# Four small transposes moved into an earlier wait, one batch's attention units one group sooner, and another cut of a tile's lead groups

## The chip, the cores and the metric

One core of one Trainium2 chip. The metric is the device time of one execution in microseconds (us). Times are quoted as medians over executions. A "mean granted clock" stands beside every execution: the share of full speed that TensorE was granted over the span. 1.000 or 0.999 is called full clock here. The span that a profile shows is about 1.8 us shorter than the device time of the same execution.

## The reference, cut to what matters

```python
# retention attention: q, k, v are (8 batches, 8 heads, 576 positions, 64)
scores = scale * q @ k.T
ret    = scores * Dmat            # gamma[h] ** (i - j) for i >= j, else 0
x      = (ret @ v) as rows of 512 # 8 * 576 = 4608 tokens

# mixture of 4 experts, all of them for each token
p   = domain_probs / (domain_probs.sum(-1) + 1e-09)
out = sum over e of  p[:, e] * (relu(x @ w1[e]) @ w2[e])   # 512 -> 1024 -> 512
```

## The kernel before

The 4608 tokens are worked through in nine tiles of 512. A tile is a Python generator `moe(nt)`: for each of 4 experts it runs 8 "up" groups (w1, one group for 128 hidden rows) and 4 "po" groups (w2, one group for 128 tokens) and yields after each, so a tile has 48 groups, counted from 0. A table `plan` names what attention work of the next batch is emitted after which group. All TensorE work is one instruction stream in the order of emission; that order is what this change edits. A batch has 576 tokens, so tile 1 (tokens 512 to 1023) needs the last 64 tokens of batch 0 and the first 448 of batch 1, chunk by chunk of 128: `xT` of batch 1's chunk 3 must be there before tile 1's last columns.

```python
def mixing_weights():                       # after group 1 of tile 0
    pp = ps_at.tile([128, E, NTT], FP32, tag="at", name="pp")
    for e in range(E):
        nc.tensor.transpose(pp[:, e, :], probs_raw[:, :, e], identf)
    nc.vector.tensor_copy(probs, pp)
    ...                                     # normalise on VectorE

def moe(nt, lead=0):
    n0 = nt * NT
    ...
    for e in range(E):
        hT = hpool.tile([128, NFC, NT], BF16, tag="hT")
        for fc in range(NFC):
            if e == 0 and fc < lead:
                if fc == 0:
                    early = [ps_mm.tile([128, NT], FP32, tag="mm", name="ph") for _ in range(lead)]
                    for x in range(lead):
                        up(early[x], e, x, slice(0, NT // 2))
                        if x != 1:
                            yield
                ph = early[fc]
                up(ph, e, fc, slice(NT // 2, NT))
            ...
            nc.scalar.activation(hT[:, fc, :], ph, Relu)
            yield
        for ns in range(NSUB):
            po = ...                        # 8 matmuls over fc, needs all of hT and w2
            ...
            yield

# start of the program, after attention of batch 0 in four units:
    next(tile0)            # half groups of tile 0, wait for the first half of w1[0]
    a0.O(*UNITS[3])
    next(tile0)
    w20 = load_w2(0)       # the DMA of the first w2 is issued on POOL, in order with the casts
    late_constants()       # with identf, the 36x36 identity for the transposes
    ...
# tile 0: batch 1's chunks. Tc transposes q and k, kv updates the state,
# Sc computes scores, Oc the output and xT
    for c, g in enumerate((40, 42, 44, 46)):
        at(g, Tc(c))
        if c < 3: at(g + 1, kv(c), Sc(c))
        if c > 0: at(g + 1, Oc(c - 1))
    at(47, kv(3))
# after tile 0:
    Sc(3); next(tiles[1]); next(tiles[1])   # three half groups of tile 1
    Oc(3)
```

Of the kernel before, what the change touches and what calls it, by code (L numbers as in the profile page):

```python
# [9 lines left out]
FP32 = mybir.dt.float32  # L10
# [10 lines left out]
def kernel(  # L21
# [10 lines left out]
    nc = tc.nc  # L32
    B, H, S, D = q.shape
    N, E = moe_domain_probs.shape
# [10 lines left out]
    NT = 512  # L45
    n_nt = N // NT
    NSUB = NT // 128
    NTT = N // 128
    lg = [math.log(1.0 - 2.0 ** (-5.0 - h)) for h in range(H)]
    allp = list(range(NP))  # L50

    const = ctx.enter_context(tc.tile_pool(name="const", bufs=1))
# [6 lines left out]
    ps_mm = ctx.enter_context(tc.tile_pool(name="ps_mm", bufs=3, space=PSUM))  # L59
    ps_at = ctx.enter_context(tc.tile_pool(name="ps_at", bufs=4, space=PSUM))  # L60
# [12 lines left out]
    state = {}  # L73
# [20 lines left out]
    def load(b):  # L94
        load_alloc(b)
        for c in range(NCH):
            load_chunk(b, c)
        load_rem(b)
# [49 lines left out]
                   allow_small_or_imprecise_dtypes=True)  # L148
    ident = const.tile([128, 128], BF16)
    make_identity(nc, ident)  # L150

    tri2 = const.tile([128, 2, 128], BF16)
    nc.gpsimd.memset(tri2, 1.0)
# [1 line left out]
        nc.gpsimd.affine_select(out=tri2[j:j + 64], in_=tri2[j:j + 64], compare_op=mybir.AluOpType.is_ge,  # L155
                                fill=0.0, base=0, channel_multiplier=-2, pattern=[[-1, 2], [1, 128]])
    tri = const.tile([128, 128], BF16)
    identf = const.tile([NTT, NTT], FP32)

    def late_constants():  # L160
        nc.gpsimd.memset(tri, 1.0)
        nc.gpsimd.affine_select(out=tri, in_=tri, compare_op=mybir.AluOpType.is_ge, fill=0.0,
                                base=0, channel_multiplier=-1, pattern=[[1, 128]])
        nc.gpsimd.tensor_copy(identf, ident[:NTT, :NTT])

    lgp = const.tile([128, NP], FP32)
    for p in range(NP):
# [11 lines left out]
    def load_gq(pairs):  # L179
        for p in pairs:  # L180
            nc.scalar.activation(gq[:, p, :], pos_i, Exp, scale=lgp[:, p:p + 1], bias=lsc)
# [5 lines left out]
    probs = const.tile([128, E, NTT], FP32)  # L187
    psm = const.tile([128, NTT], FP32)

    def mixing_weights():  # L190
        pp = ps_at.tile([128, E, NTT], FP32, tag="at", name="pp")
        for e in range(E):
            nc.tensor.transpose(pp[:, e, :], probs_raw[:, :, e], identf)
        nc.vector.tensor_copy(probs, pp)
        nc.vector.tensor_reduce(psm, probs[:, :, :].rearrange("p e t -> p t e"),
                                axis=mybir.AxisListType.X, op=ADD)
        nc.vector.tensor_scalar_add(psm, psm, 1e-9)
        nc.vector.reciprocal(psm, psm)
        nc.vector.tensor_tensor(probs, probs, psm[:, :].unsqueeze(1).to_broadcast([128, E, NTT]), op=MULT)
# [260 lines left out]
                                        gq[:, 2 * u:2 * u + 2, ts], op=MULT)  # L460


    def moe(nt, lead=0):
        n0 = nt * NT

        def up(ph, e, fc, ts):
            for dc in range(NDC):
                nc.tensor.matmul(ph[:, ts], lhsT=w1_sb[e][:, dc, fc * 128:(fc + 1) * 128],  # L468
                                 rhs=xT[:, dc, n0 + ts.start:n0 + ts.stop], start=(dc == 0), stop=(dc == NDC - 1))

        acc = [apool.tile([128, Dm], FP32, tag="acc", name="acc") for _ in range(NSUB)]
# [4 lines that stand above are left out]
                    if fc == 0:  # L476
                        early = [ps_mm.tile([128, NT], FP32, tag="mm", name="ph") for _ in range(lead)]
                        for x in range(lead):
                            up(early[x], e, x, slice(0, NT // 2))
                            if x != 1:  # L480
                                yield
                    ph = early[fc]
                    up(ph, e, fc, slice(NT // 2, NT))
                else:
                    ph = ps_mm.tile([128, NT], FP32, tag="mm", name="ph")
                    up(ph, e, fc, slice(0, NT))
# [3 lines that stand above are left out]
                t = nt * NSUB + ns  # L490
                pe = probs[:, e, t:t + 1]
                last = t == NTT - 1 and e == E - 1
                w = Dm // 2 if last else Dm
                for d in range(0, Dm, w):
                    po = ps_mm.tile([128, w], FP32, tag="mm", name="po")
                    for fc in range(NFC):
                        nc.tensor.matmul(po, lhsT=hT[:, fc, ns * 128:(ns + 1) * 128],  # L497
                                         rhs=w2_sb[e][:, fc, d:d + w], start=(fc == 0), stop=(fc == NFC - 1))
                    a = acc[ns][:, d:d + w]
                    if e == 0:  # L500
                        nc.scalar.activation(a, po, Copy, scale=pe)  # L501
                    else:
                        nc.vector.scalar_tensor_tensor(a, po, pe, a, op0=MULT, op1=ADD)  # L503
                    if e == E - 1:
                        eng = nc.scalar if last and d // w % 2 else nc.sync
                        eng.dma_start(out=out[n0 + ns * 128:n0 + (ns + 1) * 128, d:d + w], in_=a)
                yield
# [2 lines left out]
    a0 = AttP(0)  # L510
    UNITS = [(hf, u) for hf in range(2) for u in range(2)]

    tiles = [moe(nt, lead=3 if nt < 2 else 0) for nt in range(n_nt)]
    tile0 = tiles[0]
    warm(8)
    for n, eng in (("k", nc.gpsimd), ("q", nc.scalar), ("v", nc.gpsimd)):
# [1 line left out]
    for x, (hf, u) in enumerate(UNITS):  # L518
        a0.T(hf, u, nc.scalar)
        if x < 2:  # L520
            load_gq((2 + x,))
        if x == 0:
            warm(4)
        else:
            a0.O(*UNITS[x - 1])
        if x < 3:
            a0.cast("k", *UNITS[x + 1], nc.gpsimd)
            a0.cast("q", *UNITS[x + 1], nc.gpsimd)
            if x:
                load_w1(0, x - 1)  # L530
            a0.cast("v", *UNITS[x + 1], nc.gpsimd)
        a0.S(hf, u)
        if x == 0:
            warm(2)
        a0.kv(hf, u)
    next(tile0)
    a0.O(*UNITS[3])
    next(tile0)
# [11 lines left out]
    for nt in range(n_nt):  # L550
        plan = {}

        def at(g, *fs):
            plan.setdefault(g, []).extend(fs)

        if nt == 0:
            at(1, mixing_weights)
            at(3, lambda: a0.cast_rem(nc.gpsimd))
            at(20, a0.Trem)
            at(22, a0.Srem)  # L560
            at(24, a0.Orem)
            def begin1():
                A = state["a1"] = Att(1)
                for c in range(NCH):
                    for n in "kqv":
                        A.cast(n, c, nc.gpsimd)
                    if c == 0:
                        load_chunk(1, 2)
                        load_chunk(1, 3)
                load_rem(1)  # L570
                load(2)

            at(25, begin1)
            for c, g in enumerate((40, 42, 44, 46)):
                at(g, lambda c=c: state["a1"].Tc(c))
                if c < 3:
                    at(g + 1, lambda c=c: state["a1"].kv(c, allp), lambda c=c: state["a1"].Sc(c))
                if c > 0:
                    at(g + 1, lambda c=c: state["a1"].Oc(c - 1))
            at(47, lambda: state["a1"].kv(3, allp))  # L580
        elif nt + 1 < B:
            if nt == 1:
                a1 = state["a1"]
                at(0, lambda: a1.cast_rem(nc.gpsimd))
                at(2, a1.Trem)
                at(4, a1.Srem)
                at(6, a1.Orem)
            def begin(b=nt + 1):
                A = state["A"] = Att(b)
                for c in range(NCH):  # L590
                    for n in "kqv":
                        A.cast(n, c, nc.gpsimd)
                A.cast_rem(nc.gpsimd)
                for c in range(NCH + 1):
                    A.dmaT(c)
                if b + 1 < B:
                    load(b + 1)

            at(7 if nt == 1 else 0, begin)
            for n, g in zip(range(NCH), (13, 15, 17, 18) if nt == 1 else (9, 11, 13, 15)):  # L600
                at(g, lambda n=n: state["A"].kv(n, allp))
            at(19 if nt == 1 else 17, lambda: state["A"].S([0, 1]))
            at(24, lambda: state["A"].Srem(), lambda: state["A"].O([0, 1]))
            at(27, lambda: state["A"].S([2, 3]))
            at(32, lambda: state["A"].O([2, 3], rem=True))
        for g, _ in enumerate(tiles[nt]):
            for f in plan.get(g, ()):
                f()
        if nt == 0:
            state["a1"].Sc(3)  # L610
            next(tiles[1])
            next(tiles[1])
            state["a1"].Oc(3)


# [28 lines left out]
```

## Time and profile before

| | us |
|---|---|
| device time, median of 3 | 563.56 |
| span of the profiled execution | 561.2 |
| TensorE busy (98% of the span) | 552.4 |
| TensorE stall before the first `po` (w2 landing) | 0.76 |
| TensorE stall for batch 1's last `xT` | 0.78 |

The list of what TensorE waited for, in the kernel before (what it was about to do, whom it waited for, total us, times, longest):

```profile
...
PE ph L468 <- DVE xT L316: 0.8, 1, 0.8
PE po L497 <- DMA wt_491<-in_moe_w_dram: 0.8, 1, 0.8
PE pt L391 <- POOL qm L381: 0.7, 1, 0.7
PE ph L468 <- DMA wt_268<-in_moe_w_dram: 0.7, 1, 0.7
...
PE kvp L236 <- ACT sbd L241: 0.4, 1, 0.4
```

The two lines left out are waits at the start (1.3 and 0.4 us). The list adds up to about 5 us of 561, so a change of the order alone can win little. The change aims at two of them: the one for the first weights (`wt_268`, as a place to put work) and the one for `xT`.

The chain of waits between 10 and 30 us (start, us, what), which tells what the first `po` depends on:

```profile
15.51 0.55 POOL vm L381
16.06 11.17 DMA wt_491<-in_moe_w_dram
...
27.28 2.76 PE po L497 x12
```

The first w2 (`wt_491`) is issued by POOL at 16.06, is on its way for 11.17 us, and the first `po` starts when it has landed. TensorE does not appear in the chain before 27.28. The same stretch in TensorE's timeline (start, us, engine, line, operation, output and inputs, count, and in brackets the idle time before and what ended it):

```profile
16.51 0.72 PE L412 MATMUL kvp<-vm,km 64*128 64x128 bf16 x8
17.92 0.61 PE L468 MATMUL ph<-xT,wt_268 128*128 128x256 bf16 x4 [0.69 <-DMA wt_268<-in_moe_w_dram]
...
21.00 0.67 PE L193 MATMUL pp<-identf,probs_raw 36*128 36x36 f32 x4
...
27.28 7.08 PE L497 MATMUL po<-wt_491,hT 128*128 128x512 bf16 x32 [0.76 <-DMA wt_491<-in_moe_w_dram]
```

And the end of tile 0, where the half groups of tile 1 (line 468, 256 columns), `Oc(3)` (lines 309 and 314) and the second halves meet:

```profile
83.00 1.48 PE L468 MATMUL ph<-xT,wt_268 128*128 128x256 bf16 x12
84.42 0.46 PE L309 MATMUL oc<-sT,vm 128*64 128x128 bf16 x8
84.81 0.40 PE L314 MATMUL oc<-qkT,sbd 128*128 128x128 bf16 x4
85.99 1.47 PE L468 MATMUL ph<-xT,wt_268 128*128 128x256 bf16 x12 [0.78 <-DVE xT L316]
87.39 0.29 PE L248 MATMUL ptr<-ident,qrb 64*128 64x64 bf16 x4
...
92.87 7.07 PE L497 MATMUL po<-wt_491,hT 128*128 128x512 bf16 x32
```

The second halves need `xT` of chunk 3, which VectorE makes from the output matmuls that were emitted just before them. The last line is tile 1's first `po`, the mark for what was gained by then.

### The profile page before, as it was taken

How to read it: one execution, taken by the hardware profiler on the slowest of the kernel's cores; microseconds unless marked ns; L12 is line 12 of the kernel's file. 1: busy time of each engine (PE TensorE's matmuls, PEld its weight loads, DVE VectorE, ACT ScalarE, POOL GpSimd, SP SyncE). 2: the span in 40 equal slices, each digit the busy share in tenths (PEclk: the TensorE clock that was granted, in tenths of full speed). 3: DMA queues.
4: the chain of work that ended last, by engine and by line, in shares of the span. 5: the costliest groups of instructions: out<-in, count | busy, mean ns of one | idle time of the engine just before them, and what ended most of it. 6: DMA issues, size and time to landing. Idle time of an engine off the chain costs nothing.

```text
span 561.2 us, 8302 instructions
## 1 busy us (share of the span) xinstructions
PE 552.4 (98%) x3418; PEld 265.4 (47%) x3418; DVE 158.3 (28%) x267; ACT 227.6 (41%) x407; POOL 96.6 (17%) x143
## 2 busy tenths in 40 slices
PE   8899999999999999999999999999999999999997
PEld 4544464444444444444445444444444444444443
DVE  5303271243205420452025211532055202220222
ACT  6452334633362236323553336223622353335332
POOL 7611256016010600132010501060000000000000
PEclk9999999999999999999999999999999999999999
DMA  9999999590389025911594047703200100020002
GB/s 232 177 202 200 206 204 231 114 205 11 112 136 165 1 85 109 205 16 39 117 179 81 1 131 152 131 1 104 57 1 1 63 13 1 0 76 1 1 0 76
DMA packets 148150, 53.84 MB, mean 96 GB/s; under 512 B 130540, under 2 KB 142060, under 8 KB 148112
## 3 DMA queue, kind: packets, MB, share of 16 engines
q1 hardware_dynamic: 141168, 44.79, 38.7%
q0 software_dynamic: 6800, 8.39, 8.8%
q8 instruction: 27, 0.44, 0.4%
q10 hardware_dynamic: 144, 0.13, 0.1%
q14 instruction: 11, 0.09, 0.1%
HBM read 45.16 MB, written 9.44 MB: 97 GB/s over the span
## 4 chain that ended last, share of the span: by engine, by line
PE 94%; DMA 3%; POOL 1%; SPq 1%; DVE 0%; ACT 0%; issue 0%
PE po L497 44%; PE ph L468 43%; DMA wt_491<-in_moe_w_dram 2%; PE o L338 1%; PE kvp L236 1%; DMA raw_k<-in_k_dram 1%; PE o L349 1%; SPq L85 1%; POOL km L377 0%; PE orem L344 0%; PE ptc L284 0%; POOL wt_268 L119 0%; PE oc L309 0%; PE orem L355 0%; POOL vm L381 0%; POOL qm L381 0%
## 5 line engine op out<-in xcount | busy, mean ns | idle before, releaser
L487 ACT ACTIVATE hT<-ph 128x512 bf16<-128x512 f32 x288 | 171.6, 597 | 271.5 <-PE ph L468 270.1
L497 PEld LDWEIGHTS <-hT 128*128 128x128 bf16 x1160 | 112.4, 98 | 132.4 <-DMA wt_491<-in_moe_w_dram 1.2
L503 DVE SCALAR_TENSOR_TENSOR acc<-po,probs,acc 128x512 f32<-128x512 f32 (+1 forms) x109 | 81.3, 746 | 249.2 <-PE po L497 241.3
L468 PE MATMUL ph<-xT,wt_496 128*128 128x512 bf16 x288 | 66.8, 379 | 0.0
L468 PE MATMUL ph<-xT,wt_268 128*128 128x512 bf16 (+1 forms) x312 | 64.7, 363 | 1.5 <-DVE xT L316 0.8
L468 PE MATMUL ph<-xT,wt_500 128*128 128x512 bf16 x288 | 65.8, 379 | 0.0
L497 PE MATMUL po<-wt_491,hT 128*128 128x512 bf16 x288 | 64.5, 379 | 0.8 <-DMA wt_491<-in_moe_w_dram 0.8
L497 PE MATMUL po<-wt_502,hT 128*128 128x512 bf16 x288 | 64.6, 379 | 0.0
L497 PE MATMUL po<-wt_506,hT 128*128 128x512 bf16 (+1 forms) x296 | 64.1, 373 | 0.0
L468 PE MATMUL ph<-xT,wt_504 128*128 128x512 bf16 x288 | 64.1, 379 | 0.0
L497 PE MATMUL po<-wt_498,hT 128*128 128x512 bf16 x288 | 64.0, 379 | 0.0
L221 POOL TENSOR_TENSOR km<-raw_k,gk 128x512 bf16<-128x512 f32 x28 | 29.2, 1042 | 144.9 <-PE kvp L236 90.1
L468 PEld LDWEIGHTS <-wt_268 128*128 128x128 bf16 x312 | 30.0, 98 | 32.6 <-issue 0.9
L468 PEld LDWEIGHTS <-wt_504 128*128 128x128 bf16 x288 | 28.0, 98 | 33.4
L468 PEld LDWEIGHTS <-wt_500 128*128 128x128 bf16 x288 | 27.3, 98 | 31.6
L468 PEld LDWEIGHTS <-wt_496 128*128 128x128 bf16 x288 | 27.0, 98 | 28.8
L501 ACT ACTIVATE acc<-po,probs 128x512 f32<-128x512 f32 x36 | 24.7, 687 | 37.0 <-PE po L497 37.0
L223 POOL CAST vm<-raw_v 128x512 bf16<-128x512 f32 x28 | 17.2, 613 | 100.6 <-PE o L338 93.4
L241 ACT ACTIVATE sbd<-kvp 64x256 bf16<-64x256 f32 x56 | 20.8, 372 | 3.8 <-PE kvp L236 3.4
L223 POOL CAST qm<-raw_q 128x512 bf16<-128x512 f32 x28 | 17.1, 609 | 8.9 <-DMA raw_q<-in_q_dram 8.6
L358 DVE TENSOR_TENSOR xT<-o,gq 128x512 bf16<-128x512 f32 x24 | 15.5, 685 | 2.6 <-PE o L349 2.0
L236 PEld LDWEIGHTS <-km 128*128 128x128 bf16 x112 | 8.5, 98 | 7.0 <-issue 0.8
(251 smaller groups left out, 237.4 us busy)
## 6 DMA issues: line engine op xcount, KB each, us to landing
out_dram<-acc SPq DMA_DIRECT2D x35, 256.0 KB, 2.0
raw_k<-in_k_dram SPq DMA_DIRECT2D x32, 256.0 KB, 5.1
raw_q<-in_q_dram SPq DMA_DIRECT2D x32, 256.0 KB, 5.1
raw_v<-in_v_dram SPq DMA_DIRECT2D x32, 256.0 KB, 5.5
wt_268<-in_moe_w_dram POOLq DMA_DIRECT2D x2, 512.0 KB, 6.0
wt_491<-in_moe_w_dram POOLq DMA_DIRECT2D x1, 1024.0 KB, 11.2
wt_496<-in_moe_w_dram POOLq DMA_DIRECT2D x1, 1024.0 KB, 14.7
wt_498<-in_moe_w_dram POOLq DMA_DIRECT2D x1, 1024.0 KB, 20.6
```

The lines of the kernel that those rows point to most:

```text
L85: nc.sync.dma_start(out=pairs_of(state[b][n, hf])[:, h], in_=src[b, h, 256 * hf:256 * hf + 256, :].rearrange("h (p j) d -> p h (j d)", j=2))
L221: eng.tensor_tensor(o, i, gk[:, c, :].unsqueeze(2).to_broadcast([128, H, D]), op=MULT)
L223: eng.tensor_copy(o, i)
L236: nc.tensor.matmul(self.kvp[:, p, :], lhsT=flat(self.m["k"][:, n, h, :]), rhs=flat(self.m["v"][:, n, h, :]), start=(n == 0 and i == 0), st ...
L241: nc.scalar.activation(sbd[j:j + 64, n, a:z, j:j + 64], self.kvp[j:j + 64, a:z, j:j + 64], Copy)
L338: nc.tensor.matmul(o[64 * j:64 * j + 64, c * C:(c + 1) * C], lhsT=self.m["v"][:, c, 2 * p + j, :], rhs=self.sT[p][:, j, c, :], start=(c == ...
L358: nc.vector.tensor_tensor(xT[:, p, b * S:b * S + SM], o, gq[:, p, 0:SM], op=MULT)
L468: nc.tensor.matmul(ph[:, ts], lhsT=w1_sb[e][:, dc, fc * 128:(fc + 1) * 128], rhs=xT[:, dc, n0 + ts.start:n0 + ts.stop], start=(dc == 0), s ...
L487: nc.scalar.activation(hT[:, fc, :], ph, Relu)
L497: nc.tensor.matmul(po, lhsT=hT[:, fc, ns * 128:(ns + 1) * 128], rhs=w2_sb[e][:, fc, d:d + w], start=(fc == 0), stop=(fc == NFC - 1))
L501: nc.scalar.activation(a, po, Copy, scale=pe)
L503: nc.vector.scalar_tensor_tensor(a, po, pe, a, op0=MULT, op1=ADD)
```

## The change

The intent has three parts. Part 1: the four transposes of the mixing weights go to a place where TensorE waits anyway, before the first weights (the identity they need is made earlier on POOL). Part 2: batch 1's chunk units go one group sooner, so that the last output unit runs directly after tile 0, and the `xT` multiply on VectorE is covered by tile 1's lead groups. Part 3: tile 1 leads with two groups of three quarters of the columns instead of three halves.

```diff
+    identf = const.tile([NTT, NTT], FP32)                       # right after ident
+    nc.gpsimd.tensor_copy(identf, ident[:NTT, :NTT])
@@ late_constants
-        nc.gpsimd.tensor_copy(identf, ident[:NTT, :NTT])
@@
-    def mixing_weights():
-        pp = ps_at.tile([128, E, NTT], FP32, tag="at", name="pp")
+    def transposed_probs():
+        pp = ps_mm.tile([128, E, NTT], FP32, tag="mm", name="pp")
         for e in range(E):
             nc.tensor.transpose(pp[:, e, :], probs_raw[:, :, e], identf)
         nc.vector.tensor_copy(probs, pp)
+
+    def mixing_weights():
@@
-    def moe(nt, lead=0):
+    def moe(nt, lead=0, cut=NT // 2, pause=False):
@@
-                            up(early[x], e, x, slice(0, NT // 2))
-                            if x != 1:
+                            up(early[x], e, x, slice(0, cut))
+                            if pause and x != 1:
                                 yield
                     ph = early[fc]
-                    up(ph, e, fc, slice(NT // 2, NT))
+                    up(ph, e, fc, slice(cut, NT))
@@
-    tiles = [moe(nt, lead=3 if nt < 2 else 0) for nt in range(n_nt)]
+    tiles = [moe(0, lead=3, pause=True), moe(1, lead=2, cut=3 * NT // 4)] + [moe(nt) for nt in range(2, n_nt)]
@@
+    transposed_probs()
     next(tile0)
     a0.O(*UNITS[3])
@@ batch 1's chunks
-            for c, g in enumerate((40, 42, 44, 46)):
+            for c, g in enumerate((39, 41, 43, 45)):
                 at(g, lambda c=c: state["a1"].Tc(c))
-                if c < 3:
-                    at(g + 1, lambda c=c: state["a1"].kv(c, allp), lambda c=c: state["a1"].Sc(c))
+                at(g + 1, lambda c=c: state["a1"].kv(c, allp), lambda c=c: state["a1"].Sc(c))
                 if c > 0:
                     at(g + 1, lambda c=c: state["a1"].Oc(c - 1))
-            at(47, lambda: state["a1"].kv(3, allp))
+            at(47, lambda: state["a1"].Oc(3))
@@ after tile 0
-        if nt == 0:
-            state["a1"].Sc(3)
-            next(tiles[1])
-            next(tiles[1])
-            state["a1"].Oc(3)
```

More of the change, by code (lines that the diff above doesn't have):

```diff
@@ L157 @@
     tri = const.tile([128, 128], BF16)
-    identf = const.tile([NTT, NTT], FP32)
     def late_constants():
```

## The prediction

> **What bounds the kernel now.** TensorE: the page gives PE 98% busy in a 561.2 us span, and the chain of waits is 94% PE. From about 110 us on the chain is moe matmuls back to back. The list of waits shows few TensorE stalls: 1.3 us at the start, 0.45 and 0.7 us on casts, 0.7 us on the first half of the first weights (ends 17.92), 0.76 us on the first w2 (ends 27.28), 0.78 us on batch 1's last xT chunk (85.2 to 85.99), 0.36 us on an sbd copy (107.0). Only those can be won.
>
> **Part 1, transposes of the mixing weights.** The four transposes take 0.6 us on TensorE at 21.0 us (timeline). TensorE last works at 17.2 and waits to 17.92, so they fit there; the added identity copy on POOL (0.21 us) falls into POOL's idle 0.46 us before its first cast at 3.90, and probs_raw was issued at 10.0. So tile 0's up matmuls should end 0.6 us earlier, near 25.9 instead of 26.5. But the next thing needed is the first w2, which landed at 27.23; the chain runs through POOL's casts to that transfer, issued at 16.06 and 11.17 us long. Nothing in the diff moves its issue. I expect the wait before the first `po` to grow from 0.76 to about 1.4 us: gain 0.
>
> **Part 2, batch 1's units one group sooner.** Today the last chunk's output matmuls follow three half groups of tile 1 (1.42 us), and then TensorE waits 0.78 us for the xT multiply on VectorE (0.69 us). After it, those matmuls run directly after tile 0's last group and the 8 lead matmuls of 384 columns follow (about 1.3 us, estimated from 0.118 us for a 256-column and 0.216 us for a 512-column one). VectorE has the last `acc` (0.75 us) and then xT: ready about 0.9 us after the output matmuls end, inside those 1.3 us. The wait should vanish: 0.78 us. The inputs allow it: chunk casts end on POOL at 67.6, 71.3 and 75.0 (q) and 76.5 us (last v), each before its new use by my replay (69.5, 72.6, 77.7, 79.8). The tightest has about 1.3 us to spare.
>
> **Part 3, lead groups.** 24 matmuls of 256 columns (2.83 us) become 8 of 384, 8 of 128 and 4 of 512. In this trace 128-column matmuls with fresh weights come every 0.056 us (8 transposes in 0.45), so about 1.3 + 0.5 + 0.86 = 2.66: gain 0.15 us. The Trainium skill (TensorE: Matmul & The Clock Gate, Back-to-back issue gap) gives 81 ns sustained at N=128; then nothing is gained. I follow the trace.
>
> **A ceiling.** Batch 2's q/k transposes by DMA are issued by a queue that is DMA bound (last main one at 104.63, about 2.5 us to landing, so about 107.1); their first use is at 108.19. TensorE arriving over 1.0 us earlier would wait there. This may take back a tenth or two.
>
> **Sum:** -0.78 - 0.15 + about 0.05 = -0.9 us: 562.7 us, range 562.1 to 563.4. Faster by over 2%: 0.003; within 2%: 0.99; slower: 0.007.
>
> **What would show it.** List of waits: xT wait gone; `po` on first w2 about 1.4 us, ending at 27.3 again; the transposes at 17.2 to 17.9. The first `po` of tile 1, at 93.0 us today, near 92.1, and everything after 110 us shifted by the same amount.
>
> **What would make it wrong.** w2 landing earlier or later by DMA chance (moves the result one for one); the casts for batch 1 arriving later than today, so the earlier units wait; the DMA transposes holding the first score matmuls of batch 2, which gives part of the gain back; 128-column matmuls slower than 0.06 us.

## The result, and the profile after

| | before | after |
|---|---|---|
| device time, median of 6 (us) | 563.41 | 562.54 |
| lowest to highest | 562.70 to 563.93 | 561.39 to 564.35 |

The ratio is 0.9987, 95% interval 0.997 to 1.0004. A ratio here is the mean time of one kernel's runs over that of the other's of the same rounds, so not quite the ratio of the medians above. By itself this result is within noise of no change: one of the six executions of the changed kernel, at 564.35 us, had a mean clock of 0.996, and the other five lie at 561.39 to 562.71. That slow one is the execution that was profiled, so its span (562.6 us) is longer than that of before. It is still of use, since the parts can be read one by one.

What TensorE waited for in the changed kernel's first profile:

```profile
PE pt L393 <- POOL qm L383: 2.5, 3, 1.2
PE po L499 <- DMA wt_498<-in_moe_w_dram: 2.0, 1, 2.0
PE warm_out L134 <- DVE warm_in L129: 1.3, 1, 1.3
...
PE kvp L238 <- ACT sbd L243: 0.4, 1, 0.4
...
```

The wait for `xT` is gone, and so is the one for the first weights. The wait before the first `po` grew from 0.8 to 2.0 us. TensorE's timeline of the beginning:

```profile
17.51 0.67 PE L193 MATMUL pp<-identf,probs_raw 36*128 36x36 f32 x4
18.11 0.61 PE L470 MATMUL ph<-xT,wt_269 128*128 128x256 bf16 x4
...
28.01 2.30 PE L499 MATMUL po<-wt_498,hT 128*128 128x512 bf16 x6 [2.00 <-DMA wt_498<-in_moe_w_dram]
```

The transposes sit where they were meant to, and the first `po` again starts at the landing of w2. In this execution the transfers on the chain were late from the start (the chain of waits has the raw k of the third unit landing at 10.37, in before at 10.03; w2 at 27.96, in before at 27.23). And the granted clock fell right after the stall. Busy times by stretch (bounds, length, then busy us and counts of PE, PEld, DVE, ACT, POOL, then the granted clock, DMA share and GB/s):

```profile
28.20:28.40 0.20, 0.20 (x2) 0.10 (x1) 0.00 (x0) 0.00 (x0) 0.00 (x0) 1.00 1.14 215
28.40:28.60 0.20, 0.20 (x2) 0.10 (x1) 0.00 (x0) 0.00 (x0) 0.00 (x0) 0.74 1.14 215
28.60:28.80 0.20, 0.20 (x2) 0.00 (x0) 0.00 (x0) 0.00 (x0) 0.00 (x0) 0.50 1.03 195
...
31.50:31.80 0.30, 0.30 (x2) 0.04 (x1) 0.00 (x0) 0.30 (x1) 0.00 (x0) 0.50 1.17 201
31.80:32.00 0.20, 0.20 (x2) 0.15 (x1) 0.00 (x0) 0.09 (x1) 0.00 (x0) 0.73 1.17 202
```

From 28.5 to 31.9, 3.4 us long (the two stretches of 0.2 us at its edges have 0.74 and 0.73), TensorE had half its clock: the first expert's `po` groups of tile 0 took 8.55 us in the chain of waits instead of 6.91 (the value of every later round), a loss of 1.64 us. Without it this execution would have been at 562.7, an estimate.

The end of tile 0 in the same profile:

```profile
85.42 0.41 PE L311 MATMUL oc<-sT,vm 128*64 128x128 bf16 x8
85.77 0.40 PE L316 MATMUL oc<-qkT,sbd 128*128 128x128 bf16 x4
86.00 2.77 PE L470 MATMUL ph<-xT,wt_269 128*128 128x384 bf16 x19
88.71 0.29 PE L250 MATMUL ptr<-ident,qrb 64*128 64x64 bf16 x4
```

(One of its 20 records is missing.) No stall is left between `Oc(3)` and the remainder groups. From the start of the block to the first `ptr`: before, 83.00 to 87.39, 4.39 us; after, 85.42 to 88.71, 3.29 us.

### The profile page after: what moved, and what is told of

It is laid out like the page before. It is cut to its first block, busy times and chain, and to the rows that moved or that the text cites. A ratio compares the mean times of both kernels' runs of the same rounds, so it can differ in the third digit from the quotient of the medians.

```text
span 562.6 us, 8230 instructions
## 1 busy us (share of the span) xinstructions
PE 548.6 (98%) x3353; PEld 264.6 (47%) x3414; DVE 158.3 (28%) x267; ACT 227.3 (40%) x407; POOL 96.6 (17%) x143
## 4 chain that ended last, share of the span: by engine, by line
PE 93%; DMA 3%; POOL 1%; issue 1%; SPq 1%; ACT 0%; DVE 0%; ACTq 0%
PE po L499 44%; PE ph L470 43%; DMA wt_498<-in_moe_w_dram 2%; PE o L340 1%; DMA raw_k<-in_k_dram 1%; PE kvp L238 1%; PE o L351 1%; SPq L85 1%; POOL km L379 0%; PE orem L346 0%; PE ptc L286 0%; POOL wt_269 L119 0%; PE oc L311 0%; PE orem L357 0%; POOL vm L383 0%
## 5 line engine op out<-in xcount | busy, mean ns | idle before, releaser
L470 PE MATMUL ph<-xT,wt_502 128*128 128x512 bf16 x275 | 65.3, 379 | 0.5
L470 PE MATMUL ph<-xT,wt_506 128*128 128x512 bf16 x281 | 65.3, 379 | 0.4
L470 PE MATMUL ph<-xT,wt_269 128*128 128x512 bf16 (+3 forms) x298 | 63.8, 365 | 0.5
L470 PE MATMUL ph<-xT,wt_510 128*128 128x512 bf16 x286 | 64.0, 379 | 0.2 <-issue 0.2
```

Source lines behind the costliest of these rows:

```text
L470: nc.tensor.matmul(ph[:, ts], lhsT=w1_sb[e][:, dc, fc * 128:(fc + 1) * 128], rhs=xT[:, dc, n0 + ts.start:n0 + ts.stop], start=(dc == 0), s ...
```

## The experiments

Two theories stood against each other. Theory W: the landing of the first w2 is a gate; nothing that TensorE saves before it counts, so part 1 gains nothing and parts 2 and 3 are the whole gain. Rival R: the transposes were on the path, and part 1 is worth its 0.6 us. A third, theory C, came from the first profile: the longer stall that part 1 causes makes the half-clock stretch likely, so part 1 may even cost. A measure that does not depend on when w2 lands, used throughout, is the time from the start of the first `po` to the start of tile 1's first `po` in TensorE's timeline: 92.87 - 27.28 = 65.59 us before. Every experiment was timed in five rounds beside the kernel before; the eleven kernels ran in three groups, each group on a chip of its own (medians of before there: 563.11, 563.19, 563.36).

### 1. The changed kernel again

No edit.

> The changed kernel unaltered, for more executions on the same chip as the next three. Theory W (the landing of the first w2 gates all that comes before it, so that the moved transposes gain nothing and parts 2 and 3 are the whole gain): about 1.0 us under the kernel before in executions at full clock. Theory C (the longer stall before the first po sometimes costs one half-clock stretch of about 3.4 us): some executions, perhaps one in six, about 1.6 us longer at a mean clock of 0.996 or 0.997, the others at 0.999 or above. If the dip in the first profile was mere chance of that chip, no such execution here.

Median 561.91 us, ratio 0.9973 (0.9955 to 0.9991). The five executions at full clock average 561.80 against 563.14 for the ten of before at full clock, a gain of 1.34 us. The sixth had a mean clock of 0.994 and yet took only 562.40: a low clock where TensorE waits for DMA anyway would cost nothing, but this execution has no trace to show where it fell. Of the eleven executions of before, one took 566.15 us at 0.996. So the dip also visits the kernel before, and the part of theory C that blames the change is in doubt. The timeline of this second profile, which is at full clock:

```profile
27.12 4.06 PE L499 MATMUL po<-wt,hT 128*128 128x512 bf16 x18 [1.45 <-DMA wt<-in_moe_w_dram]
...
82.85 0.41 PE L311 MATMUL oc<-sT,vm 128*64 128x128 bf16 x8
83.20 0.40 PE L316 MATMUL oc<-qkT,sbd 128*128 128x128 bf16 x4
83.43 2.77 PE L470 MATMUL ph<-xT,wt 128*128 128x384 bf16 x20
86.14 0.29 PE L250 MATMUL ptr<-ident,qrb 64*128 64x64 bf16 x4
...
91.61 7.07 PE L499 MATMUL po<-wt,hT 128*128 128x512 bf16 x32
```

The stall before the first `po` is 1.45 us, close to the 1.4 predicted, and the first `po` of tile 1 starts at 91.61: 64.49 us after the first `po`, 1.10 less than before.

### 2. Part 1 alone

```diff
 kernel before, with
+    identf and its copy right after ident;  transposed_probs() before the first next(tile0)
-    the same in late_constants and in mixing_weights
```

> The kernel before with part 1 alone (transposes moved to the wait for the first weights, identity copied earlier). Theory W: same time as before, ratio 1.000 within 0.001; in the trace the tile's last up matmul ends about 0.6 us sooner, the wait before the first po grows from 0.8 to 1.4 to 2.0 us, and the first po starts when w2 lands as ever. Rival R (the transposes were on the critical path): 0.6 us faster. Theory C adds: slower on average than before if some executions drop to half clock after the longer stall.

Median 563.28 us, ratio 0.9997 (0.998 to 1.0014). One execution had a mean clock of 0.996; at 563.62 it took no longer than the others. Its timeline:

```profile
17.30 0.67 PE L193 MATMUL pp<-identf,probs_raw 36*128 36x36 f32 x4
18.57 0.61 PE L470 MATMUL ph<-xT,wt 128*128 128x256 bf16 x4 [0.60 <-DMA wt<-in_moe_w_dram]
...
28.14 3.19 PE L499 MATMUL po<-wt,hT 128*128 128x512 bf16 x14 [1.67 <-DMA wt<-in_moe_w_dram]
```

The stall is longer (1.67), the first `po` starts at the landing of w2 as ever, and from there to tile 1's first `po` it is 65.60 us, as before. The times alone would not decide: rival R's 0.6 us is a ratio of 0.9989, inside the interval. With the trace, and with experiment 7, theory W holds for part 1 and rival R falls.

### 3. Parts 2 and 3 without part 1

```diff
 changed kernel, with the transposes back in mixing_weights and the identity back in late_constants
```

> Parts 2 and 3 without part 1 (transposes left at 21 us). Theory W: the whole gain, about 1.0 us under before, wait before the first po about 0.8 to 1.3 us as in before, first po to tile 1's first po about 64.7 us (before 65.75). Rival R: only 0.4 us of gain or so, 0.6 behind the changed kernel. Theory C: no half-clock execution, since the stall is not lengthened.

Median 562.08 us, ratio 0.9989 (0.9966 to 1.0012). Two of six executions had clocks of 0.997 and 0.996 and took 564.08 and 564.95; the other four average 561.95, a gain of 1.19 over before at full clock. In its trace:

```profile
27.41 7.08 PE L497 MATMUL po<-wt,hT 128*128 128x512 bf16 x32 [1.06 <-DMA wt<-in_moe_w_dram]
...
91.90 7.07 PE L497 MATMUL po<-wt,hT 128*128 128x512 bf16 x32
```

From first `po` to tile 1's first `po` it is 64.49 us, to the hundredth that of the changed kernel. So parts 2 and 3 are the whole gain. (This interval of the ratio holds both theories, too; it is the trace that tells them apart.) Theory C is wrong where it said that this kernel would be spared: its stall is shorter (1.06 us), and it dipped in two of six, the most of this group.

### 4. The first w2 in two halves

If the landing is the gate, TensorE should be given work that needs only half of w2. The transfer is split by rows, and the first three `po` groups run their first four matmuls before any needs the second half.

```diff
-        return nc.gpsimd.dma_start(out=wt2, ...)
+        n = NFC // parts                       # parts = 2 for the first w2
+        for x in range(parts):
+            i = nc.gpsimd.dma_start(out=wt2[:, x * n:(x + 1) * n, :], ...)   # rows x*512 to (x+1)*512
+        return i
@@ moe, tile 0, first expert, before the loop over ns
+                for ns in range(3):
+                    ahead.append(ps_mm.tile([128, Dm], FP32, tag="mm", name="po"))
+                    for fc in range(NFC // 2):
+                        nc.tensor.matmul(ahead[ns], lhsT=hT[:, fc, ns * 128:(ns + 1) * 128],
+                                         rhs=w2_sb[e][:, fc, :], start=(fc == 0), stop=False)
@@ the groups 0 to 2 then go on in ahead[ns] with fc from NFC // 2
```

> The changed kernel with the first w2 loaded as two transfers of half its rows, and the first three po groups of tile 0 starting with the four matmuls that need only the first half (12 matmuls, 2.6 us), the rest after. Theory W: the first half lands some 3 us before the second, so TensorE fills the wait: 1.4 to 2.0 us under the changed kernel, about 2.5 to 3 us under before, stall before the first po near 0. If what follows is limited by DMA elsewhere (batch 1's chunks at 65 to 76 us), part of that shows up again as waits there, on casts of batch 1. Theory C: no half-clock execution.

Median 561.83 us, ratio 0.9974: no better than the changed kernel of the same rounds (561.91). That missed the expectation by about 1.5 us. The profiled execution, at 562.90 us the slowest of its six, shows a gain that was made and then lost:

```profile
25.82 2.75 PE L500 MATMUL po<-wt,hT 128*128 128x512 bf16 x12
...
90.43 7.07 PE L510 MATMUL po<-wt,hT 128*128 128x512 bf16 x32
...
108.32 0.45 PE L269 MATMUL s<-qkT 64*128 64x128 bf16 x10 [2.23 <-DMA qkT<-km]
```

`po` starts at 25.82 with no stall (the first half of w2 landed at 24.42, the second at 27.34), and tile 1's first `po` at 90.43 instead of 91.61. Then the first score matmuls of batch 2, which run after group 19 of tile 1, wait 2.23 us for a transpose that the DMA queues make. The prediction had named this ceiling. The chain of waits in that stretch shows the queue of SyncE issuing (SPq) and the last transfer on the chain:

```profile
104.53 1.21 SPq L261
...
105.79 2.48 DMA qkT<-km
...
108.32 0.45 PE s L269 x10
```

Those ten transposes are issued one after the other, about 1.25 us each, by a queue that here is paced by the transfers and a cast ahead of it: between 89.95 and 108.32 no TensorE work is on the chain. An earlier TensorE only waits for them. But the 2.23 us are not all due to that. The transpose landed at 108.27 in this execution and at 107.09 in the kernel before; at that time about 1.05 us of the wait would be left, an estimate, against the 1.18 us gained by tile 1's first `po`. The two nearly cancel, which is what the median shows.

### 5. Halves, and the scores two groups later

```diff
-            for n, g in zip(range(NCH), (13, 15, 17, 18) if nt == 1 else (9, 11, 13, 15)):
+            for n, g in zip(range(NCH), (13, 15, 17, 19) if nt == 1 else (9, 11, 13, 15)):
                 at(g, lambda n=n: state["A"].kv(n, allp))
-            at(19 if nt == 1 else 17, lambda: state["A"].S([0, 1]))
+            at(21 if nt == 1 else 17, lambda: state["A"].S([0, 1]))
```

> The kernel with the first w2 in halves, and in tile 1 the last state update of batch 2 at group 19 (was 18) and its first score matmuls at group 21 (was 19), so that the DMA transposes of batch 2 have 3.4 us more. Theory D (in the run with w2 in halves the gain was real, 2 to 3 us up to tile 1's first po, and was given back at the wait for the DMA transposes, 2.2 us in its trace): now the gain stays: about 559.3 us, 3.5 to 4 us under before, 2.3 to 2.6 under the kernel with halves, no TensorE wait between 20 and 115 us above 0.3 us. Rival (something else, such as total DMA traffic, sets the time of the first 110 us): the wait only moves, time stays near 561.8.

Median 560.50 us, ratio 0.9954 (0.9941 to 0.9967), 2.7 us under before: in the direction of theory D, short of its 3.5 to 4. One execution, the profiled one, had a clock of 0.996 and took 562.15. In its trace the half-clock stretch fell into the up groups (from 19.6 to 23.1 us). TensorE waited for nothing from 20 to 120 us. The edit also removed the wait of 0.36 us for the copy `sbd`, which the changed kernel has before the last state update (`kvp`, now one group later), so not all of the gain belongs to the opened gate. The later scores without the halves were not run.

### 6. Three half groups as the lead of tile 1 (part 3 undone)

```diff
-    tiles = [moe(0, lead=3, pause=True), moe(1, lead=2, cut=3 * NT // 4)] + ...
+    tiles = [moe(0, lead=3, pause=True), moe(1, lead=3)] + ...
```

> The changed kernel, but tile 1 led as before by three half groups (24 matmuls of 256 columns instead of 8 of 384, 8 of 128 and 4 of 512). If the saving of part 3 is the smaller number of matmuls, this is 0.15 to 0.25 us slower than the changed kernel, about 562.1 us, still without a wait for xT (the three halves take 1.4 us, xT needs about 0.9). If the cut is what makes the wait go (xT too late for halves), a wait for xT of some tenths comes back.

Median 562.15 us, ratio 0.9983; two of five executions at a clock of 0.997, the three at full clock average 561.98. The changed kernel did not run in this group, so the trace decides. The lead block is one line:

```profile
83.87 2.78 PE L470 MATMUL ph<-xT,wt 128*128 128x256 bf16 x24
86.59 0.29 PE L250 MATMUL ptr<-ident,qrb 64*128 64x64 bf16 x4
```

24 matmuls in 2.72 us, where the changed kernel takes 2.71 for its 20 (83.43 to 86.14), no wait for `xT`, and from first `po` to tile 1's first `po` (27.57 to 92.06) again 64.49 us. Part 3 is worth nothing (0.01 us in the lead block), and the whole 1.10 us is part 2.

### 7. The stall filled with dummy matmuls

```diff
+            if nt == 0 and e == 0:
+                warm(6)                        # 6 matmuls of 512 columns, result unused
             for ns in range(NSUB):
```

> The changed kernel with six dummy matmuls of 512 columns (1.3 us, result unused) between the last up matmul of tile 0's first expert and its first po. Theory W: same time as the changed kernel (561.9 in executions at full clock), because they run in the stall for w2, which shrinks from 1.4 to 2.0 us to 0.1 to 0.7. Rival R (work before the w2 landing counts): 1.3 us slower. Theory C: no half-clock execution; but with one in six to one in twelve so far this can't be told from chance by six executions.

Median 562.29 us, ratio 0.9985 (0.9972 to 0.9998), all five executions at full clock. Their mean, 562.34, is 0.88 under before of the same rounds, where the changed kernel gains 1.34 and 1.25 in the two other groups. Six extra matmuls, which took 1.46 us in the timeline (25.75 to 27.21), cost at most a few tenths, as far as two chips can be compared. In the trace the `po` starts at 27.27, at the landing of w2 (the chain has it at 27.22): TensorE has 1.4 us to give away here.

### 8. The first w2 delayed

```diff
+    load_w1(1, 0)                              # half of the second expert's w1 ahead of w2[0]
     w20 = load_w2(0)
     ...
     for e in range(1, E):
-        load_w1(e)
+        load_w1(e, 1 if e == 1 else None)
```

> The changed kernel with half of the second expert's w1 loaded ahead of the first w2, so that w2 lands about 3 us later and the stall before the first po grows to 4.5 to 5 us. Theory W: 3 us slower than the changed kernel in executions at full clock, one for one, about 565 us. Theory C (long stalls cost a stretch of half clock): most or all executions show a mean clock of 0.997 or less and about 1.6 us more, so near 566.5; if the dips have nothing to do with the stall, one or none of six.

Median 566.49 us, ratio 1.0059. All five executions had clocks of 0.993 to 0.997. In the profiled one w2 landed at 29.34, about 2 us later than usual and not 3, so the stall was 3.53 us, less than expected:

```profile
29.39 8.77 PE L499 MATMUL po<-wt,hT 128*128 128x512 bf16 x32 [3.53 <-DMA wt<-in_moe_w_dram]
```

The half clock followed it (columns as in the first profile after the change):

```profile
30.50:33.50 3.00, 3.00 (x9) 1.14 (x8) 0.00 (x0) 0.69 (x1) 0.00 (x0) 0.53 1.24 207
```

So with a stall of about 3.5 us, seen in one trace, the mean clock fell in five of five, and with the shorter stalls of the other kernels only now and then. The median is just what theory C forecast, but partly by luck: a delay of 2 us and one stretch of half clock explain the profiled 565.73, not the longer ones up to 567.68, which have no trace. The Trainium skill (TensorE: Matmul & The Clock Gate, What's actually happening) describes this: TensorE's clock is halved by default and released by activity, judged in free-running windows of about 3.4 us. Three traces hold such a stretch: this one, the first of the changed kernel, and that of experiment 5. In their clock records it lasts 3.413 us each time and follows 23.893, 23.893 and 13.653 us of full clock, which is 7, 7 and 4 times 3.413, so lengths and places agree with such windows. The window just before the stretch held 1.26 us of drawn TensorE work here and 1.42 in the changed kernel; the emptiest window around a stall of 1.45 to 1.71 us held 1.70, and full clock followed. In experiment 5's trace it held 2.64 and the stretch came all the same, so busy time alone does not decide. The windows begin at another time in each execution (full clock begins at 4.60 us of the span in the changed kernel's first trace, at 7.15 in the second), which could be why one stall of a kernel brings the stretch and the next does not; that is argued, not tested.

### 9 to 11. The comparison on one chip, and part 1 where the gate is gone

The changed kernel, the kernel of experiment 5, and that kernel without part 1:

```diff
 kernel of experiment 5, with the transposes back in mixing_weights and the identity back in late_constants
```

> The changed kernel unaltered, for a comparison on one chip with the two that follow: about 562.0 us in executions at full clock, first po to tile 1's first po 64.5 us.

> The kernel with w2 in halves and the scores of batch 2 two groups later, again: about 1.6 to 2.0 us under the changed kernel of the same rounds (its stall of 1.4 to 1.6 us before the first po and the 0.36 us before the last state update are gone), about 560.2 us, in executions at full clock.

> The same as the one before, without part 1: the transposes of the mixing weights back at 21 us. Theory W says that part 1 gains nothing only because the w2 landing hides it; with w2 in halves TensorE no longer stalls there, so now part 1 is worth its 0.6 us: this kernel 0.6 us slower than the one before, about 560.8. If part 1 is worth nothing in itself (for example because the first weights' landing absorbs it), no difference.

| kernel | median us | ratio to before (95%) | first `po` starts | tile 1's first `po` starts |
|---|---|---|---|---|
| changed kernel | 562.35 | 0.9984 (0.9972 to 0.9997) | 27.69 | 92.18 |
| halves, scores later | 559.96 | 0.9944 (0.9931 to 0.9956) | 25.34 | 89.93 |
| the same, transposes late | 560.38 | 0.9948 (0.9936 to 0.9961) | 26.07 | 90.54 |

The starts are those of each kernel's one profiled execution. The timeline of the last two (first the one with part 1, then without):

```profile
17.61 0.61 PE L474 MATMUL ph<-xT,wt 128*128 128x256 bf16 x4
...
25.34 2.75 PE L500 MATMUL po<-wt,hT 128*128 128x512 bf16 x12
```

```profile
17.60 0.61 PE L472 MATMUL ph<-xT,wt 128*128 128x256 bf16 x4 [0.24 <-DMA wt<-in_moe_w_dram]
...
20.70 0.67 PE L197 MATMUL pp<-identf,probs_raw 36*128 36x36 f32 x4
...
26.07 2.75 PE L498 MATMUL po<-wt,hT 128*128 128x512 bf16 x12
```

Both start on the first weights at 17.6, so the transposes (at 17.00 in the first) cost nothing in the wait; the one that runs them at 20.7 reaches its `po` 0.73 us later and tile 1's first `po` 0.61 us later. The medians differ by 0.42 us, the means of all executions by 0.2 (560.25, with one execution of 561.87 at full clock that has no trace, and 560.45), so the timed difference is within the intervals, and one trace of each carries the verdict: once the gate is gone, part 1 gains about its own length up to tile 1's first `po`. That all of it lasts to the end is not shown. The kernel of experiment 5 beats both: 3.4 us under before and 2.4 under the changed kernel by medians. It is the best version found.

## Why the prediction was right

The measured median, 562.54 us, lies in the predicted range of 562.1 to 563.4, near 562.7. That alone says little, since the kernel before, with 563.41 in the same rounds, lies at the edge of that range. What shows the prediction right are the parts:

- Part 1, "gain 0": right, and for the reason given. Alone it measured 0.9997. The stall before the first `po` became 1.45 to 1.71 us in the four profiles at full clock that have part 1 and wait for the whole w2, and 2.00 in the first one (predicted about 1.4). What was too rigid was "ending at 27.3 again": w2 landed between 27.1 and 28.1 us over the profiles that left its load alone, and that scatter goes into the time one for one, as the prediction said under what would make it wrong.
- Part 2, "0.78 us": right in mechanism, too small in size. It measured 1.10 us. Between the start of `Oc(3)` and the restart of the lead groups there are 1.57 us before (84.42 to 85.99) and 0.58 after (82.85 to 83.43), so 0.99 us came from there. The list of waits showed 0.78 because it counts from the end of the last matmul. A 128-column matmul is drawn 0.22 us long although such matmuls follow each other every 0.056 us; the last one before a stall is drawn in full as busy time, which hides 0.16 us of the stall. By starts the wait is about 0.94 us: the last output matmul starts at 84.99, the next matmul could have followed at 85.05 and came at 85.99. The Trainium skill (Perfetto Trace Analysis, Tensor Engine Instruction) says that these ends are estimated, and the 0.16 us agrees with reading starts rather than ends. The rest of the 0.99 is `Oc(3)` itself, whose first eight matmuls take 0.39 us before (84.42 to 84.81) and 0.35 after. The other 0.11 us of the 1.10 is the two bursts of 12 matmuls (1.42 and 1.40 us) that became one block of 2.71.
- Part 3, "gain 0.15 us": wrong, and the term that was mis-sized is the old block, not the new cut. In the changed kernel's second trace, 8 matmuls of 128 columns take 0.45 us (narrow windows of the timeline put the first at 84.73 and the 512-column one after the last at 85.18), 0.056 each, as the prediction had it; the 81 ns at N=128 that the Trainium skill gives (TensorE: Matmul & The Clock Gate, Back-to-back issue gap) did not hold here. The 384-column ones take 1.30, so with 4 of 512 at 0.216 the block is 2.61 us, near the predicted 2.66. But the 256-column matmuls of experiment 6 follow each other every 0.109 us, 24 in 2.62, where the prediction took 0.118 and 2.83. Its 0.118 is a burst of 12 in 1.42 us, which holds the change to the next operation: the last matmul of a burst is followed after 0.20 us instead of 0.109 (84.22 to 84.42). Both blocks pay that once (2.71 and 2.72 us in the timeline), the kernel before paid it twice. So joining the bursts, which comes with part 2, saved about 0.1 us, and the new cut 0.01. The errors of size in parts 2 and 3 cancelled in part: 0.93 predicted, 1.10 measured. That is luck.
- The ceiling: not reached by the changed kernel (no wait for the DMA transposes in any of its three profiles; in the second TensorE came 1.26 us earlier than before, and the transpose landed at 106.31 instead of 107.09), but reached as soon as the w2 gate was opened, at 2.2 us (experiment 4), and removed by moving the scores (experiment 5).
- Not foreseen: the half-clock stretch. It cost the first profiled execution 1.64 us, and it widened the first interval until the result looked like no change. By the mean of executions at full clock, the changed kernel gained 1.34 and 1.25 us in the two later groups. So that the first median, with one slowed execution among six, came so near to 562.7 owes something to chance.

What stays open: how much of experiment 5's gain (2.7 and 3.4 us by medians in two groups) the halves and the later scores each brought; and whether a stall of 1 to 2 us raises the odds of a dip. Counting a mean clock of 0.997 or less, the kernel before, with 0.76 us, dipped in 1 of 33 executions of the three groups, parts 2 and 3 alone, with 1.06 us, in 2 of 6, the changed kernel in 3 of 17, part 1 alone in 1 of 6, the kernel of experiment 6 in 2 of 5. One kernel alone is too few to tell. Taken together, those with a stall of 1.06 to 2.00 us before the first `po` dipped in 8 of 34, and those with none or 0.76 in 2 of 61 (the kernel before, experiments 4, 5, 7, 10 and 11). If the stall made no difference, so uneven a split would have a chance of about 0.004 (Fisher's exact test), but the grouping was made after the runs, and most of these dips have no trace that shows where they fell. So it points to yes and does not prove it.

## What to carry to other kernels

Before moving work out of a busy stretch, follow the chain to the next thing that the engine needs from elsewhere: what is saved ahead of a transfer that has not landed only lengthens the wait for it, unless the first work after it is rearranged to need only what is there. When such a gate is opened, look at once for the next consumer of a transfer that is paced by its own queue, and move that consumer too. Size a TensorE stall by the starts of the instructions around it, and compare executions at the same granted clock when the effect is under one per cent.

## What the Trainium skill lacked or had wrong

- TensorE: Matmul & The Clock Gate, What's actually happening: the clock falls "after ≥1 idle window (~3.4µs)". The half-clock stretch does last 3.4 us here (28.5 to 31.9), but the window before it was not idle: in one execution the stretch followed a stall of 2.00 us, with 1.42 us of TensorE work in the 3.41 before it. With a stall of 3.53 us in the trace, the mean clock fell in five of five executions; after 1.45 to 1.71 us the stretch came in none of four traces. No page gives odds for stalls shorter than a window.
- TensorE: Matmul & The Clock Gate, Back-to-back issue gap: 81 ns sustained at N=128 with fresh weights. In this kernel eight transposes came in 0.45 us (0.056 each), and so did the eight remainder matmuls of 128 columns. For N=512 it gives about 131 ns sustained and about 216 isolated; the steady rounds here show 32 in 6.91 us, 0.216 each. So at both sizes the figure that the section calls isolated is the one that held back to back.
- Perfetto Trace Analysis, Tensor Engine Instruction, says that the end is estimated, but not what follows for a stall: here the listed wait of 0.78 us stood for about 0.94 us by the starts.
